# Batch 0's first feed-forward phase: w_in's first quarter in two loads, norms ahead of q's second part, single token tiles

## The chip, the cores and the metric

The kernel runs on one core of one Trainium2 chip. Times are microseconds (us) measured on the device, the whole program each time. The runs of one experiment were made together on one chip, experiments 2 and 3 on other chips than 1 and 4, so times are compared within an experiment. A profile is one such execution with every instruction recorded; its span is 1.7 to 2.1 us shorter than the time of the same run.

Names in the profile: PE is TensorE's matmuls and PEld its weight loads, DVE is VectorE, ACT is ScalarE, POOL is GpSimd (which here mostly issues loads). L453 is a line of the kernel; the changed kernel and most experiments have the same line a few numbers later (L456), as lines were added above it.

## The reference, cut to what matters

```python
def phi(x):                                     # elu(x) + 1
    return np.where(x > 0, x, np.exp(x) - 1.0) + 1.0
q_p, k_p = phi(q), phi(k)                       # batch 8, heads 8, seq 576, head_dim 64
kv  = np.einsum('bhsd,bhse->bhde', k_p, v)
z   = np.sum(k_p, axis=2)
num = np.einsum('bhsd,bhde->bhse', q_p, kv)
den = np.einsum('bhsd,bhd->bhs', q_p, z)[..., None] + 1e-06
x   = (num / den)  # -> (4608, 512)
h   = x @ w_in                                  # 512 x 2048
g   = h * (1 / (1 + np.exp(-beta * h)))
out = g @ w_out                                 # 2048 x 512
```

## The kernel before

It works batch by batch. For each batch, linear attention gives x, transposed to xT. The "H phase" multiplies xT by w_in and puts a silu on the result; the "y phase" multiplies by w_out. PE runs batch 0's H and y phases while batch 1's attention is prepared between their matmuls. Everything is in a fixed order that the program gives. The loads all go through one queue that GpSimd issues:

```python
    load_nine(k9, k)
    load_nine(q9, q, j1=4)
    ...                                         # batch 0's v
    load_nine(q9, q, j0=4)
    for i in range(4):
        nc.gpsimd.dma_start(out=w_in_sb[i], in_=w_in_v[:, :, i * 512 : (i + 1) * 512])
    load_w_out(0)
    load_w_out(1)
    load_k(1)
    load_q(1)
    ...
    load_w_out(2)
    load_v(1)
    load_w_out(3)
```

The start of batch 0's H phase, and the plan of what is slipped in after which group (a group is four matmuls: one 128-wide slice ff of w_in's columns times token tiles t0 to t1):

```python
    exp0(0, 4, N9)
    relu0(0, 4, N9)
    silu_table()
    num_norm(0, 0)                              # VectorE: den, reciprocal, multiply -> xs
    phi0(0, 4, 6)
    warm(4)                                     # matmuls on zeros
    x_trans(0, 0, dve=True)                     # PE transposes xs, VectorE copies it to xT
    qb2 = att_banks(BF16)
    q_trans0(2, qb2, 0)
    q_out0(2, qb2, 0, False)
    num_norm(0, 1)
    phi0(0, 6, N9)
    ...
    h_phase(
        0, xT[0],
        [(ff, 0, 1) for ff in range(4)] + [(ff, 1, 2) for ff in range(4)]
        + [(ff, 0, 2) for ff in range(4, 8)] + [(ff, 2, 4) for ff in range(8)]
        + [(ff, 0, 4) for ff in range(8, 12)],
        {
            3: [F(x_trans, 0, 1), F(num_mm, 0, 2), F(num_norm, 0, 2), F(q_rest0)],
            5: [F(num_mm, 0, 3), F(num_norm, 0, 3)],
            7: [F(x_trans, 0, 2)],
            8: [F(num_mm, 0, 4), F(num_norm, 0, 4)],
            9: [F(x_trans, 0, 3), F(tidy0)],
            12: [F(x_trans, 0, 4)],
            17: [F(w_out_scale, 0), F(w_out_scale, 1)],
        },
    )
```

And what comes after it:

```python
    h_last(0, xT[0], [])                        # the last four ff of the H phase
    ...
    exp_(1, 1); exp_(1, 0)                      # ScalarE, batch 1's k and q
    silu_table()
    relu(1, 1); relu(1, 0)                      # VectorE from here
    w_out_scale(2)
    phi(1, 1)                                   # the minimum, k
    v_copy(1)                                   # vaug <- vraw: needs v(1)'s load
    phi(1, 0)                                   # the minimum, q
    y_phase_wide(0, {
        ...
        9: [F(kv_mm, 1), F(kv_evac, 1), F(w_out_scale, 3)],
        10: [F(q_trans, 1, 0, 1, wide=True), F(q_trans, 1, 2, 3, wide=True)],
        ...
    })
```

## Time and profile before

| | |
|---|---|
| time, median of 3 | 296.88 us (296.63 to 297.01) |
| span of the profile | 295.1 us |
| PE busy | 285.1 us, 97% |
| first matmul of the H phase | 17.09 us |
| first matmul of the y phase | 34.09 us |
| batch 1's kv matmuls start | 42.82 us |

Here is VectorE at the start of the H phase, from the instructions in order of time (start in us, length in us, engine, line, what it writes and reads; in brackets the idle time before it and what ended it). The first norm (den, rden, xs) starts only when relu0, the first row, is done, although its own inputs were there; that is the order the change turns round.

```profile
13.76 0.65 DVE L264 TENSOR_SCALAR r<-xqk 128x1280 bf16<-128x1280 bf16 x1 [0.55 <-DMA xqk<-in_q_dram]
14.45 0.17 DVE L413 TENSOR_SCALAR den<-att 128x8 f32<-128x8 f32 x1
14.88 0.69 DVE L415 TENSOR_TENSOR xs<-att,rden 128x512 bf16<-128x512 f32 x1
16.07 0.42 DVE L370 COPY xT<-mm 128x512 bf16<-128x512 bf16 x1 [0.16 <-PE mm L433]
```

And two lines of the waits of PE and its weight loads (total us, times, longest): the wait that the change is after, and one, much smaller in the list.

```profile
PE mm L453 <- DMA w_in<-in_moe_w_in_dram: 0.8, 1, 0.8
PEld L344 <- DVE vaug L370: 0.4, 1, 0.4
```

### The profile page before, as it was taken

Reading aid. Unit: us, or ns where it says so; the run is one execution under the profiler, and the core shown is the slowest. Engines: PE = TensorE matmul, PEld = TensorE weight load, DVE = VectorE, ACT = ScalarE, POOL = GpSimd, SP = SyncE. Lnnn points to the kernel's source line nnn. Section 1 sums busy time; section 2 is a strip of 40 time slices with the busy share of each in tenths; the row PEclk is TensorE's granted clock in tenths of the full one; section 3 lists DMA queues with packets and bytes.
Section 4 is the critical chain, followed back from the end, with each engine's and each line's share of the span. In section 5 each row is a group of like instructions: output and inputs, shape, how many; then the busy total and the mean of one; then the engine's idle time right before and its main releaser. Section 6 shows DMA issues by size and latency. Waiting matters only on the chain.

```text
span 295.1 us, 4791 instructions
## 1 busy us (share of the span) xinstructions
PE 285.1 (97%) x1911; PEld 144.9 (49%) x1932; DVE 125.2 (42%) x264; ACT 175.5 (59%) x234; POOL 52.2 (18%) x72
## 2 busy tenths in 40 slices
PE   8979999999999999999999999999999999999994
PEld 2557445644565544445444544454445444444443
DVE  5675388504772174616461646164715400110012
ACT  2798786889988770778077808790770077018500
POOL 8925475544006000320020000000000000000000
PEclk9999999999999999999999999999999999999998
DMA  7999999999939943698357445024502400120032
GB/s 109 189 205 344 255 273 192 257 193 190 164 142 150 180 93 98 130 177 151 98 128 79 73 116 126 2 72 115 127 0 73 117 36 0 38 94 13 2 71 71
DMA packets 69719, 36.43 MB, mean 123 GB/s; under 512 B 38321, under 2 KB 64193, under 8 KB 69697
## 3 DMA queue, kind: packets, MB, share of 16 engines
q0 software_dynamic: 38912, 20.45, 47.7%
q1 hardware_dynamic: 30624, 15.55, 21.0%
q8 instruction: 15, 0.25, 0.4%
q10 hardware_dynamic: 160, 0.13, 0.2%
q14 instruction: 8, 0.06, 0.0%
HBM read 36.71 MB, written 9.44 MB: 156 GB/s over the span
## 4 chain that ended last, share of the span: by engine, by line
PE 71%; DMA 17%; ACT 4%; POOL 4%; issue 3%; DVE 0%; POOLq 0%; ACTq 0%
PE mm L453 33%; PE mm L505 32%; DMA xqk<-in_q_dram 9%; DMA vraw<-in_v_dram 4%; DMA w_in<-in_moe_w_in_dram 4%; PE att L399 2%; ACT e L229 2%; POOL xqk L131 1%; PE att L344 1%; PE mm L537 1%; ACT L229 1%; POOL vraw L131 1%; ACT g L445 1%; POOL w_in L159 1%; ACT L445 0%
## 5 line engine op out<-in xcount | busy, mean ns | idle before, releaser
L445 ACT ACTIVATE g<-mm,beta_c 128x512 bf16<-128x512 f32 (+2 forms) x156 | 97.3, 633 | 88.1 <-PE mm L453 87.8
L505 PE MATMUL mm<-w_out,g 128*128 128x512 bf16 x541 | 127.2, 379 | 1.2 <-issue 0.3
L453 PE MATMUL mm<-xT,w_in 128*128 128x512 bf16 (+2 forms) x560 | 107.8, 349 | 1.2 <-DMA w_in<-in_moe_w_in_dram 0.8
L453 PEld LDWEIGHTS <-w_in 128*128 128x128 bf16 x656 | 62.0, 98 | 62.0 <-DMA w_in<-in_moe_w_in_dram 1.0
L505 PEld LDWEIGHTS <-g 128*128 128x128 bf16 x560 | 52.7, 98 | 57.3
L515 DVE COPY y_sb<-mm 128x512 f32<-128x512 f32 x27 | 18.7, 692 | 70.4 <-PE mm L505 67.4
L229 ACT ACTIVATE e<-xqk 128x2560 bf16<-128x2560 bf16 x14 | 31.9, 2329 | 0.1
L415 DVE TENSOR_TENSOR xs<-att,rden 128x512 bf16<-128x512 f32 (+1 forms) x40 | 27.6, 689 | 1.6 <-DVE rden L414 0.2
L242 DVE TENSOR_TENSOR qk_p<-r,e 128x2560 bf16<-128x2560 bf16 x14 | 20.9, 1490 | 13.1 <-ACT e L229 12.4
L355 DVE CAST kv_bd<-att 64x130 bf16<-64x130 f32 x28 | 8.2, 292 | 34.5 <-PE att L344 34.1
L72 POOL DMA_DIRECT2D vraw<-in_v_dram x7 | 6.8, 972 | 77.4 <-DVE vaug L370 70.9
L413 DVE TENSOR_SCALAR den<-att 128x8 f32<-128x8 f32 (+1 forms) x40 | 6.5, 162 | 27.0 <-PE att L399 26.8
L399 PEld LDWEIGHTS <-q_pT 128*128 128x128 bf16 (+1 forms) x160 | 11.7, 100 | 10.7 <-DVE xs L415 2.1
L399 PE MATMUL att<-kv_bd,q_pT 128*128 128x130 bf16 (+1 forms) x160 | 15.8, 221 | 1.1 <-DVE kv_bd L370 0.7
L453 PE MATMUL mm<-xT_tail,w_in 128*128 128x512 bf16 x63 | 13.9, 379 | 0.1
L237 DVE TENSOR_SCALAR r<-xqk 128x2560 bf16<-128x2560 bf16 x14 | 11.9, 858 | 3.9 <-DMA xqk<-in_q_dram 2.3
L572 PE MATMUL mm<-g 128*128 128x512 bf16 x34 | 10.4, 468 | 1.2 <-DVE g L143 1.2
L72 POOL DMA_DIRECT2D xqk<-in_k_dram x7 | 8.0, 1150 | 10.2 <-ACT e L229 3.6
L229 ACT ACT_TABLE_LOAD x7 | 9.0, 1283 | 0.1
L414 DVE RECIPROCAL rden<-den 128x8 f32<-128x8 f32 (+1 forms) x40 | 8.1, 201 | 1.4
L72 POOL DMA_DIRECT2D xqk<-in_q_dram x7 | 6.5, 924 | 6.9 <-ACT g L445 2.1
L256 ACT ACTIVATE e<-xqk 128x1280 bf16<-128x1280 bf16 (+1 forms) x4 | 4.4, 1154 | 5.1 <-DMA xqk<-in_k_dram 4.6
(72 smaller groups left out, 142.5 us busy)
## 6 DMA issues: line engine op xcount, KB each, us to landing
out_dram<-y_sb SPq DMA_DIRECT2D x28, 256.0 KB, 2.3
xqk<-in_k_dram POOLq DMA_DIRECT2D x7, 512.0 KB, 10.7
xqk<-in_q_dram POOLq DMA_DIRECT2D x7, 512.0 KB, 11.8
vraw<-in_v_dram POOLq DMA_DIRECT2D x7, 512.0 KB, 11.5
w_in<-in_moe_w_in_dram POOLq DMA_DIRECT2D x4, 512.0 KB, 11.3
g<-in_moe_w_out_dram POOLq DMA_DIRECT2D x4, 512.0 KB, 10.9
out_dram<-y_sb SPq DMA_DIRECT2D x14, 128.0 KB, 5.1
xqk<-in_moe_w_out_dram POOLq DMA_DIRECT2D x2, 512.0 KB, 14.3
```

Source lines behind the costliest of these rows:

```text
L72: eng.dma_start(out=dst[:, :, 0:NJ, :].rearrange("p h j d -> p h (j d)"), in_=src[b, :, 0:MAIN, :].rearrange("h (p j) d -> p h (j d)", j=NJ),)
L229: nc.scalar.activation(st[b, "e", a][:, h0:h1], xqk[b % NX][:, a, h0:h1], ACTF.Exp)
L237: nc.vector.tensor_scalar(st[b, "r", a][:, h0:h1], xqk[b % NX][:, a, h0:h1], 0.0, 1.0, ALU.max, ALU.add)
L242: nc.vector.tensor_tensor(st[b, "p"][:, a].rearrange("p j (h d) -> p h j d", h=H)[:, h0:h1], st[b, "r", a][:, h0:h1], st[b, "e", a][:, h0: ...
L355: nc.vector.tensor_copy(kv_bd[b % 2][i][gs, :, g, :], st[b, "kvp"][gs, 2 * i : 2 * i + 2, :])
L399: nc.tensor.matmul(nps[:n, p // 2, c0 : c0 + 2 * (D + 1)], st[b, "qT"][:, t, p, :n], kv_bd[b % 2][p // 2][:, p % 2], start=True, stop=True ...
L415: nc.vector.tensor_mul(xs[:n], nv[:, :, :, 0:D], rden[:n, :, :, None].to_broadcast([n, 2, 4, D]))
L445: nc.scalar.activation(g_sb[b % 2][:, ff, c0:c1], hp[:, c0:c1], ACTF.Silu, scale=beta_c[:, ff : ff + 1],)
L453: nc.tensor.matmul(hp[:, c0:c1], w_in_sb[ff // 4][:, kc, (ff % 4) * P : (ff % 4 + 1) * P], x[:, t0:t1, kc, :] if b < B else x[:, kc, c0:c1 ...
L505: nc.tensor.matmul(yp, g_sb[b % 2][:, ff, t * P : (t + 1) * P], w_out_sb[ff // 4][:, ff % 4, :], start=(ff == 0), stop=(ff == FC - 1),)
L515: nc.vector.tensor_copy(y_sb, yp)
L572: nc.tensor.matmul(st["warm"], g_sb[0][:, FC - 1, 0:P], g_sb[0][:, FC - 1, :], start=True, stop=True, skip_group_check=True,)
```

## The change

The intent: PE stood still for 0.88 us for the first norm and 0.84 us for w_in. So load half a quarter of w_in first, let VectorE do the norm ahead of relu, move q's second part (which would hold PE, ScalarE and VectorE up ahead of the first H matmuls) into the H phase, and take the last token tiles later and one by one, so that H groups never wait for two tiles at once. The diff, cut to its core:

```diff
-    for i in range(4):
-        nc.gpsimd.dma_start(out=w_in_sb[i], in_=w_in_v[:, :, i * 512 : (i + 1) * 512])
+    for f0, f1 in ((0, 256), (256, 512), (512, 1024), (1024, 1536), (1536, 2048)):
+        i, c0 = f0 // 512, f0 % 512
+        nc.gpsimd.dma_start(
+            out=w_in_sb[i][:, :, c0 : c0 + f1 - f0], in_=w_in_v[:, :, f0:f1]
+        )
...
     exp0(0, 4, N9)
-    relu0(0, 4, N9)
     silu_table()
     num_norm(0, 0)
-    phi0(0, 4, 6)
+    relu0(0, 4, N9)
     warm(4)
     x_trans(0, 0, dve=True)
-    qb2 = att_banks(BF16)
-    q_trans0(2, qb2, 0)
-    q_out0(2, qb2, 0, False)
+    warm(2)
     num_norm(0, 1)
-    phi0(0, 6, N9)
+    phi0(0, 4, 6)
...
-        + [(ff, 0, 2) for ff in range(4, 8)] + [(ff, 2, 4) for ff in range(8)]
+        + [(ff, 0, 2) for ff in range(4, 8)] + [(ff, 2, 3) for ff in range(4)]
+        + [(ff, 3, 4) for ff in range(4)] + [(ff, 2, 4) for ff in range(4, 8)]
         + [(ff, 0, 4) for ff in range(8, 12)],
         {
-            3: [F(x_trans, 0, 1), F(num_mm, 0, 2), F(num_norm, 0, 2), F(q_rest0)],
-            5: [F(num_mm, 0, 3), F(num_norm, 0, 3)],
-            7: [F(x_trans, 0, 2)],
-            8: [F(num_mm, 0, 4), F(num_norm, 0, 4)],
-            9: [F(x_trans, 0, 3), F(tidy0)],
-            12: [F(x_trans, 0, 4)],
-            17: [F(w_out_scale, 0), F(w_out_scale, 1)],
+            3: [F(x_trans, 0, 1, dve=True), F(phi0, 0, 6, N9), F(q_second0)],
+            5: [F(num_mm, 0, 2), F(num_norm, 0, 2), F(q_rest0)],
+            8: [F(num_mm, 0, 3), F(num_norm, 0, 3)],
+            9: [F(x_trans, 0, 2)],
+            10: [F(num_mm, 0, 4), F(num_norm, 0, 4), F(tidy0)],
+            12: [F(x_trans, 0, 3)],
+            15: [F(x_trans, 0, 4)],
+            25: [F(w_out_scale, 0), F(w_out_scale, 1)],
         },
```

`q_second0` holds the three lines about `qb2`.

More of the change, by code (lines that the diff above doesn't have):

```diff
@@ L636, in tidy0, with q_second0 @@
         nc.vector.memset(vraw[0][TAIL:P, :, NJ, :], 0.0)
+    def q_second0():
+        st["qb2"] = att_banks(BF16)
+        q_trans0(2, st["qb2"], 0)
+        q_out0(2, st["qb2"], 0, False)
     def q_rest0():
+        qb2 = st["qb2"]
         q_trans0(3, qb2, 256)
```

## The prediction

> **What bounds the kernel now.** I read the page's first part, then the chain that ended last, then each engine's instructions in order of time from 13 to 46 us, where the change acts, and last the windows of DMA traffic. One core, so no dies to compare; PEclk is 9 or 10 tenths throughout.
>
> ```profile
> PE 285.1 (97%) x1911; PEld 144.9 (49%) x1932; DVE 125.2 (42%) x264; ACT 175.5 (59%) x234; POOL 52.2 (18%) x72
> PE 71%; DMA 17%; ACT 4%; POOL 4%; issue 3%; DVE 0%; POOLq 0%; ACTq 0%
> ```
>
> PE is busy 97% of the span, and the chain is PE 71%, its last 213 us (from 82.1) nearly all matmuls back to back. All of the change lies before 34 us, so it can pay only if PE reaches the unchanged part earlier and nothing there makes it wait again. The start, PE:
>
> ```profile
> 13.73 1.02 PE L572 MATMUL mm<-g 128*128 128x512 bf16 x4
> 15.63 0.40 PE L433 MATMUL mm<-identity,xs 128*128 128x128 bf16 x4 [0.88 <-DVE xs L415]
> 17.09 1.07 PE L453 MATMUL mm<-xT,w_in 128*128 128x128 bf16 x16 [0.84 <-DMA w_in<-in_moe_w_in_dram]
> 19.21 0.61 PE L453 MATMUL mm<-xT,w_in 128*128 128x128 bf16 x8 [0.31 <-ACT xT L372]
> 19.93 0.39 PE L399 MATMUL att<-kv_bd,q_pT 128*128 128x130 bf16 x4
> 24.12 6.68 PE L453 MATMUL mm<-xT,w_in 128*128 128x256 bf16 x44
> 34.09 8.80 PE L505 MATMUL mm<-w_out,g 128*128 128x512 bf16 x39
> ```
>
> Columns are start, length, what, and the idle time before it with its releaser. The first H group waits 0.84 us for the whole first quarter of w_in; its input tile was ready earlier (copy 16.07 to 16.49). This H phase runs from 17.09 to 34.09, 17.0 us, of which its matmuls alone are 64 x 215.5 ns = 13.8 us. Next, what meets PE after that:
>
> ```profile
> 41.88 0.83 DVE L370 COPY vaug<-vraw 128x2560 bf16<-128x2560 bf16 x1 [0.94 <-DMA vraw<-in_v_dram]
> 42.62 1.48 DVE L242 TENSOR_TENSOR qk_p<-r,e 128x2560 bf16<-128x2560 bf16 x1
> 44.02 1.20 DVE L355 CAST kv_bd<-att 64x130 bf16<-64x130 f32 x4
> 42.82 0.82 PE L344 MATMUL att<-vaug,qk_p 128*64 128x65 bf16 x40
> 44.45 0.61 PE L380 MATMUL att<-identity,qk_p 128*128 128x128 bf16 x8
> 45.28 0.62 PE L380 MATMUL att<-identity,qk_p 128*128 128x128 bf16 x8 [0.22 <-DVE kv_bd L355]
> ```
>
> This is the main finding. Batch 1's kv matmuls start at 42.82, just after the copy of v(1) ends at 42.71, and that copy waited 0.94 us for v(1)'s **load**. PE without that wait would be there at 34.09 + 40 x 0.2155 = 42.71. So PE and the loads arrive together to about 0.1 us. From the copy on, VectorE runs without a gap (copy, minimum, kv_bd eviction), and PE waits for that eviction at 45.28. PE's schedule from 45.28 on is therefore set by when v(1) lands, not by when the H phase ended.
>
> v(1)'s landing is set by the traffic. In the windows from 12 us to 42 us the DMA part shows all slices at 9, and the landings come in issue order: w_in's quarters are seen at POOL's releases at 17.34, 19.76, 22.35 and 24.88, some 2.55 us each. The queue is never empty: POOL issues v(1) at 28.88 and it lands about 41.8.
>
> **What the Trainium skill says.** (1) "ScalarE: Activation LUTs", What ACT_TABLE_LOAD costs: an ACTIVATE with one pointer operand takes about 280 ns + 0.833 ns per column, back-to-back ones overlap by 93 ns, a table load takes about 1283 ns. The trace has 0.69 us for a 512-wide silu (page: 0.71), 0.47 for 256 (0.49), four of 128 in 1.14, and 1.28 for the table load: it agrees. So narrow groups are dear on ScalarE. (2) "TensorE: Matmul & The Clock Gate", Wait — 56ns, not 53.3ns?: warm matmuls follow at 55.6 ns for 128 columns and 215.7 for 512. Here 16 of 128 columns take 0.91 us to the next instruction, 57 ns each: narrow groups are cheap on PE. (3) "DMA: Bandwidth & Descriptors", Specifications: line rate needs 512 B or more. Half a quarter has rows of 256 bf16, 512 B, just at that limit; k's main load has the same rows. (4) "Trainium Kernel Development and Optimization", Best Practices, point 5: matmul busy share is a poor measure. Agreed here: PE reads 5.00 of 5.00 us between 20 and 25, though the steps below find about 0.5 us of waiting there.
>
> **The change part by part.**
>
> *w_in's first quarter in two loads.* The first half should land one half of 2.55 us before the whole did, about 15.8; the second at 17.1 or slightly later. From the packets' starts, 1,024 B packets of w_in pass at about 100 per 0.5 us and 512 B packets of k(1) at about 194. So 1,024 half-size packets take 2.64 us and 512 whole ones 2.55: everything behind comes **0.09 us later**. One more issue of 0.75 us on POOL is hidden, with several loads queued.
>
> *The norm ahead of relu.* The first norm waited behind relu0 (13.76 to 14.45); its own inputs were ready at about 13.7. Now den starts there, xs is ready at 13.7 + 1.12 + 0.06 = 14.87 instead of 15.63. But relu (0.65 us) now stands between xs and the copy to xT, so that copy starts at about 15.4 and the H matmuls could start at 15.9 instead of 16.55. The first half of w_in is there.
>
> *The H groups.* ff 0 and 1 of tile 0 run at 15.90 to 16.36. Then ff 2 needs the **second** half: 17.15. So ff 0 to 3 end at 17.15 + 2 x 0.228 = 17.61 instead of 18.00. Of the 1.2 us earlier start only 0.4 survive.
>
> *q's second part* moves into the H phase: 8 small transposes, 0.2 us of PE, earlier done in the wait for w_in. xT's second copy on VectorE ends at 18.46 instead of 19.15; the second tile starts at about 18.5 instead of 19.21, a gain of 0.7. Then num_mm of tile 2 and q's rest (0.38 + 0.30) stand ahead of its last two groups. num_mm of tile 3 waits for the last q copy, since its PSUM buffer is that of the q transposes (in the trace it starts at 19.93 as that copy ends at 19.92); in the new order that is about 20.65. I follow PE, ScalarE and VectorE step by step this way with the durations above (a silu every 0.25, 0.39, 0.62 us for 128, 256, 512 columns; a copy to xT 0.47). At the end of ff 7 of tiles 0 and 1 PE is at 22.8, against 23.1 in the same walk through the kernel before, which had also done one more transposition of 0.23. The lead is gone.
>
> *Single token tiles.* Four groups of 256 columns become eight of 128. PE: 4 x (2 x 0.228 - 0.432) = +0.10 us. ScalarE: 4 x (2 x 0.2525 - 0.39) = **+0.46 us**. Between 23 and 25.5 ScalarE owes eight silus of 0.25 and copies of 0.47 and 0.38, 2.9 us, for PE work of 8 x 0.228 + 0.45 = 2.3. With four PSUM banks shared by groups and transposes, PE then waits for a bank, about 0.6 us in all.
>
> *The sum for the H phase.* The walk ends at 33.89 for the kernel before (measured 34.09) and at 34.30 for the changed one: the phase ends **0.4 us later**, near 34.5, with PE at the kv matmuls at about 43.12, 0.30 late. w_out_scale sits later in the plan but holds the same place in VectorE's order, and waits for loads anyway: nothing.
>
> *What of it reaches the end.* A late kv ends at about 43.94; VectorE is free for the eviction only at 44.02 + 0.09. The 0.30 fits into the 0.34 (44.02 - 43.68) that lay there. What is left is the 0.09 of the loads. 296.88 + 0.09 = **296.97**.
>
> **The rivals.** *A: the early start carries through.* For it: the two waits 0.88 and 0.84 vanish in part. If the second half landed soon enough, or my bank waits were wrong, PE would leave the H phase up to 0.6 us earlier. Against it: v(1) lands when it lands, so at most about 0.1 us comes through, 296.8. Only if v(1)'s landing moved too could more be had, to about 296.3. *B: ScalarE becomes the bound in the single-tile stretch and PE is later than I find.* Each 0.1 us past the slack goes straight to the end. With an H phase 0.9 us longer, the time would be about 297.4. For it: four PSUM banks, and xT copies queued behind silus. Against: VectorE took one copy away from ScalarE. *C: the halves slow the traffic* by more than packet counts say, a pause between two transfers of say 0.3 us (a guess): everything behind it, v(1) included, shifts, 297.2. *D: a gain or loss over 2%*, 5.9 us: PE's waits in the changed stretch amount to some 2.5 us, so a gain of that size is not there to have; a loss would need a new wait longer than any named here.
>
> **Range and chances.** The three runs of before span 0.4 us. My centre is 297.0. Downwards there is only A and noise: 296.4. Upwards B and C: 297.7. Faster by over 2%: 0.01; slower: 0.01; within 2%: 0.98.
>
> **What would show each step right or wrong.** First H matmul near 15.9, and an idle PE of about 0.8 us before ff 2, released by w_in near 17.1. If ff 2 starts by 16.5, the two-halves step is wrong. PE waiting on ScalarE or on banks between 23 and 26, and the first matmul of L505's successor (y) near 34.5: if it is at 34.1 or earlier, the ScalarE step is wrong. v(1)'s copy on VectorE at 41.9 to 42.0 and the kv_bd eviction at 44.1: if that copy moves earlier by more than 0.2, the main finding is wrong. From the second pair of q transposes (45.28 before) to the end, the same length to 0.2 us. The prediction fails if PE's lateness exceeds the slack, or if later waits between 45 and 82 us turn out to hang on the H phase itself.

## The result, and the profile after

The changed kernel took 297.56 us (median of 4, 296.85 to 298.03) against 296.94 for the kernel before (296.63 to 297.04). Ratios here are the mean time of one kernel's fast runs over that of the other's of the same rounds, so not quite the ratio of the medians: 1.002, 95% interval 0.9998 to 1.0043. It was run twice more: 297.21 against 296.66 (ratio 1.0012, 0.9994 to 1.003), and 296.91 against 296.87 (0.9999, 0.9986 to 1.0013). The same within 2%, and not told apart from no change at all.

At this size the record itself sets a limit. Each run's span is recorded beside its time, and what lies outside the span is 1.72 to 1.84 us in the kernel before and 1.87 to 1.98 us in the changed one. So over 0.1 us of what separates their times lies outside anything that a profile shows, and its cause is open.

The profile of the changed kernel has a span of 296.1 us. Its page and chain, for the two lines that the prediction opens with:

```profile
PE 286.1 (97%) x1929; PEld 145.7 (49%) x1950; DVE 125.0 (42%) x265; ACT 175.5 (59%) x237; POOL 53.7 (18%) x73
PE 70%; DMA 22%; ACT 2%; issue 2%; POOL 1%; DVE 0%; POOLq 0%
```

PE in the changed stretch, in order of time:

```profile
15.70 0.40 PE L436 MATMUL mm<-identity,xs 128*128 128x128 bf16 x4
16.62 0.61 PE L456 MATMUL mm<-xT,w_in 128*128 128x128 bf16 x8
18.26 0.62 PE L456 MATMUL mm<-xT,w_in 128*128 128x128 bf16 x8 [1.03 <-DMA w_in<-in_moe_w_in_dram]
19.62 0.62 PE L456 MATMUL mm<-xT,w_in 128*128 128x128 bf16 x8 [0.30 <-DVE xT L373]
35.42 8.80 PE L508 MATMUL mm<-w_out,g 128*128 128x512 bf16 x39
```

The wait for the norm is gone, and the first two groups (16.62, eight matmuls) start ahead of w_in's second half. Then PE waits 1.03 us for that half. And PE, VectorE around batch 1's kv:

```profile
42.94 0.83 DVE L373 COPY vaug<-vraw 128x2560 bf16<-128x2560 bf16 x1 [0.63 <-DMA vraw<-in_v_dram]
43.68 1.48 DVE L245 TENSOR_TENSOR qk_p<-r,e 128x2560 bf16<-128x2560 bf16 x1
45.09 1.20 DVE L358 CAST kv_bd<-att 64x130 bf16<-64x130 f32 x4
44.15 0.82 PE L347 MATMUL att<-vaug,qk_p 128*64 128x65 bf16 x40
45.78 1.18 PE L383 MATMUL att<-identity,qk_p 128*128 128x128 bf16 x16
```

Everything here lies 1.06 us later than in the kernel before (the copy of v(1) at 42.94 against 41.88), and so does the end: 296.1 against 295.1. But most of this run's delay is older than the change. The first exp waits for batch 0's k, the first load of all. These two rows are that exp (with the two that follow it) in the kernel before and, below it, in the changed one:

```profile
6.81 3.16 ACT L256 ACTIVATE e<-xqk 128x1280 bf16<-128x1280 bf16 x3 [4.57 <-DMA xqk<-in_k_dram]
```

```profile
7.98 3.17 ACT L259 ACTIVATE e<-xqk 128x1280 bf16<-128x1280 bf16 x3 [5.75 <-DMA xqk<-in_k_dram]
```

k landed 1.17 us later here, though up to that point the two programs issue the same loads in the same order. So the first question was whether that is chance, and the second what the change costs when it is taken out.

One reading of all 14 profiles carries the rest. In each of them the time from the start of the kv_bd eviction (VectorE's copy of what the kv matmuls gave) to the end of the span is between 250.97 and 251.17 us. So in these runs whatever happened before that eviction reached the end only through the moment when it started.

### The profile page after: what moved, and what is told of

Same layout as the page of the kernel before. It is cut to its first block, busy times and chain, and to the rows that moved or that the text cites. A ratio compares the mean times of both kernels' runs of the same rounds, so it can differ in the third digit from the quotient of the medians.

```text
span 296.1 us, 4832 instructions
## 1 busy us (share of the span) xinstructions
PE 286.1 (97%) x1929; PEld 145.7 (49%) x1950; DVE 125.0 (42%) x265; ACT 175.5 (59%) x237; POOL 53.7 (18%) x73
## 4 chain that ended last, share of the span: by engine, by line
PE 70%; DMA 22%; ACT 2%; issue 2%; POOL 1%; DVE 0%; POOLq 0%
PE mm L456 33%; PE mm L508 32%; DMA xqk<-in_q_dram 9%; DMA vraw<-in_v_dram 5%; DMA w_in<-in_moe_w_in_dram 4%; DMA xqk<-in_k_dram 4%; PE att L402 2%; PE att L347 1%; PE mm L540 1%; POOL xqk L131 1%; ACT e L232 1%; ACT g L448 1%; ACT L232 0%; ACT L581 0%; PE att L436 0%
## 5 line engine op out<-in xcount | busy, mean ns | idle before, releaser
L72 POOL DMA_DIRECT2D xqk<-in_k_dram x7 | 6.9, 982 | 9.2 <-ACT e L232 4.4
```

The lines of the kernel that those rows point to most:

```text
L72: eng.dma_start(out=dst[:, :, 0:NJ, :].rearrange("p h j d -> p h (j d)"), in_=src[b, :, 0:MAIN, :].rearrange("h (p j) d -> p h (j d)", j=NJ),)
```

## The experiments

The theory: the eviction starts at the later of two moments, v(1)'s copy plus 2.14 us (copy and second minimum on VectorE without a gap) or the start of the kv matmuls plus 0.87 us. The first hangs on the loads, the second on PE's H phase; the end is 251.05 us later. The rivals: PE alone sets the end; or the halved load slows the traffic; or ScalarE with its single tiles makes PE later than the slack allows. The constants were read from the first six profiles; the other eight are a test of them.

### 1. Both kernels again, and the change with and without its load

The first two are the kernels as they are. The third is the kernel before with only this:

```diff
-    for i in range(4):
-        nc.gpsimd.dma_start(out=w_in_sb[i], in_=w_in_v[:, :, i * 512 : (i + 1) * 512])
+    for f0, f1 in ((0, 256), (256, 512), (512, 1024), (1024, 1536), (1536, 2048)):
+        ...
```

The fourth is the changed kernel with these lines turned back.

> The kernel before, unchanged, as a control. Theory S (start jitter): the changed kernel's profile shows the first k load 1.2 us later than the kernel before (first exp at 7.98 against 6.81 us) although nothing ahead of it differs; so the moment the first exp starts varies from run to run, and this profile may show anything from 6.8 to 8.0, with the end moving with it. Time 296.6 to 297.1 if only this kernel's usual spread holds. Rival C2 (the change causes the late start, for instance through where things lie in memory or one more queued load): here the first exp starts at 6.8 to 6.9 and the spread of the five times stays below 0.5 us.

> The changed kernel, unchanged, to size the spread. Theory S: median within 0.4 us of the kernel before, first exp anywhere from 6.8 to 8.0; in its profile the copy of v(1) and everything after it moves with the load stream, and the time from that copy to the end is the same 253.2 us as in the first two profiles (295.1 - 41.88 and 296.1 - 42.94). Rival C2: first exp again near 8.0 and a median 0.5 us or more above the kernel before.

> The kernel before with w_in's first quarter in two loads and nothing else. Prediction's step: the traffic behind it comes 0.09 us later, so 297.0. Rival C (the halves slow the traffic by more): 297.2 to 297.6, and the spacing from the first half's landing to the second's is well over 1.3 us. The H matmuls of ff 0 and 1 start as soon as the first half is there (16.5), ff 2 waits for the second.

> The changed kernel with w_in's first quarter in one load. Theory of the prediction: 296.9, since its later H phase (0.4 us) is still swallowed before the kv_bd eviction. If the halves were what costs 0.6 us (rival C), this is at the kernel before or below; if the order of the H phase costs it (rival B), this stays at 297.5.

| kernel | median us | ratio to before (95%) | first exp | w_in complete, matmuls go on | first y matmul | v(1)'s copy | kv matmuls | eviction | span |
|---|---|---|---|---|---|---|---|---|---|
| before, first profile | 296.88 | | 6.81 | 17.09 | 34.09 | 41.88 | 42.82 | 44.02 | 295.1 |
| before again | 296.84 | 1.0003 (0.9982 to 1.0025) | 7.38 | 17.12 | 34.11 | 41.75 | 42.84 | 43.89 | 294.9 |
| changed, first profile | 297.56 | 1.002 (0.9998 to 1.0043) | 7.98 | 18.26 | 35.42 | 42.94 | 44.15 | 45.09 | 296.1 |
| changed again | 297.21 | 1.0012 (0.9994 to 1.003) | 7.19 | 17.45 | 34.62 | 41.87 | 43.34 | 44.21 | 295.2 |
| only the two loads | 297.01 | 1.0006 (0.9989 to 1.0024) | 6.93 | 17.12 | 33.66 | 41.90 | 42.79 | 44.05 | 295.1 |
| changed, one load | 297.05 | 1.001 (0.9992 to 1.0027) | 6.96 | 16.78 | 34.39 | 42.48 | 43.37 | 44.63 | 295.6 |

What follows. The late first load is not the change's doing. The two profiles of the kernel before have the first exp at 6.81 and 7.38, the first two of the changed one at 7.98 and 7.19; in experiment 2 a variant of the kernel before has it at 8.05. So rival C2 falls as to the load. The times are less clean: 297.21 is 0.55 us above the 296.66 of the kernel before in these rounds, where I had expected no more than 0.4 and C2 at least 0.5; but the same kernel's other runs beside it, as a control, had 296.84. 11 runs of the kernel before in these rounds spread from 296.29 to 298.12.

From the moment w_in is complete to the first y matmul the kernel before takes 17.00 and 16.99 us, the changed one 17.16 and 17.17. With only the two loads it is 16.54: that part alone does bring PE 0.4 us ahead. Nor do the halves slow the traffic as rival C has it: w_in is complete at 17.12, as in the control, and v(1)'s copy starts at 41.90, against 41.88 and 41.75. The halves did come 2.55 us apart, one of C's marks, but because the first landed sooner. Yet the kernel with only the two loads is not faster, since its copy of v(1) starts at 41.90 as before, and the kv matmuls at 42.79. PE could have been there at 33.66 + 8.62 = 42.28 (8.62 us are forty y matmuls of 215.5 ns); it waits 0.5 us instead (by the profile's own record of idle PE, 0.33):

```profile
42.79 0.82 PE L347 MATMUL att<-vaug,qk_p 128*64 128x65 bf16 x40 [0.33 <-DVE vaug L373]
```

In the second profile of the changed kernel it is the other way round: kv at 43.34 + 0.87 = 44.21, the eviction's start, while v(1)'s copy would have allowed 44.01. Here the later H phase came through with 0.2 us:

```profile
41.87 0.83 DVE L373 COPY vaug<-vraw 128x2560 bf16<-128x2560 bf16 x1 [0.35 <-DMA vraw<-in_v_dram]
42.61 1.49 DVE L245 TENSOR_TENSOR qk_p<-r,e 128x2560 bf16<-128x2560 bf16 x1
44.21 1.21 DVE L358 CAST kv_bd<-att 64x130 bf16<-64x130 f32 x4
```

The fourth run takes the two halves of the change apart. With one load and the new order the stretch is 17.61 us (16.78 to 34.39). So the two loads take 0.46 us off it and the new order with its single tiles adds 0.61; that comes to 0.15, and the whole change measures 0.17. Its median, 297.05, lies between the 296.9 that I had expected and the 297.5 of rival B; in its profile v(1) set the eviction (42.48 + 2.14 = 44.62, measured 44.63).

### 2. The last tiles in pairs again; more and fewer loads ahead of v(1)

First, the changed kernel with its last quarter's groups joined:

```diff
-        + [(ff, 0, 2) for ff in range(4, 8)] + [(ff, 2, 3) for ff in range(4)]
-        + [(ff, 3, 4) for ff in range(4)] + [(ff, 2, 4) for ff in range(4, 8)]
+        + [(ff, 0, 2) for ff in range(4, 8)] + [(ff, 2, 4) for ff in range(8)]
...
-            12: [F(x_trans, 0, 3)],
-            15: [F(x_trans, 0, 4)],
-            25: [F(w_out_scale, 0), F(w_out_scale, 1)],
+            11: [F(x_trans, 0, 3)],
+            13: [F(x_trans, 0, 4)],
+            21: [F(w_out_scale, 0), F(w_out_scale, 1)],
```

> The changed kernel with the last quarter's token tiles in pairs again (8 groups of 256 columns, no single tiles there), everything else of the change kept. Read from the profile: the length from the release of w_in's second half to the first y matmul. The kernel before has 17.00 and 16.99 us from its only w_in release, the changed one 17.16 and 17.17. ScalarE step (four groups split cost 0.46 us of ScalarE and bank waits on PE): 16.7 or less here. Rival (the splitting is free, the extra comes from the order of q's second part): 17.1 or more. Time about 297.0 either way, as the eviction of batch 1's kv_bd decides.

Second, the kernel before with an idle load ahead of v(1):

```diff
     load_w_out(2)
+    nc.gpsimd.dma_start(out=pad, in_=w_out_v[:, 10:12, :])     # a buffer nobody reads
     load_v(1)
```

> The kernel before with one more load of 512 KB that nobody reads, ahead of v(1). In all six profiles so far the time from the start of the kv_bd eviction to the end of the span is 250.97 to 251.08 us, and that eviction starts 2.14 us after the copy of v(1) starts. If v(1)'s landing sets the end, one load of 1.29 us more moves the copy to about 43.2, the eviction to 45.3 and the time to 298.1. If PE sets the end (rival A), the load is hidden: 296.8.

Third and fourth, both kernels with one load of the same size left out. Their outputs are wrong, which doesn't matter for the times.

```diff
+    nc.vector.memset(w_out_f[2][1], 0.0)                       # at the start
...
-    load_w_out(2)
+    nc.gpsimd.dma_start(out=w_out_f[2][0], in_=w_out_v[:, 8:10, :])
     load_v(1)
```

> The kernel before with half of w_out's third quarter not loaded (filled with zeros at the start, so a wrong result on purpose): v(1) lands 1.29 us sooner. The eviction then starts when kv's matmuls are done, 0.87 us after their start, which PE reaches by itself at the first y matmul + 8.62 = 42.72. Theory: eviction at 43.6, time 296.3 to 296.5, 0.4 less, and no more than that. If PE were not waiting for v(1) at all: 296.8. If the loads were all: 295.6.

> The same lighter loads (wrong result on purpose) in the changed kernel. Theory: the eviction waits for PE, first y matmul (34.6) + 8.62 + 0.87 = 44.1, so the time stays near 297.0, some 0.5 us above the same kernel without the change, since here nothing hides the later H phase. If the H phase is not later in truth and only the landing differs, it comes down to 296.4 like the other.

| kernel | median us | ratio to before (95%) | first y matmul | v(1)'s copy | kv matmuls | eviction | span |
|---|---|---|---|---|---|---|---|
| pairs | 297.18 | 0.9995 (0.998 to 1.0011) | 34.84 | 42.37 | 43.56 | 44.52 | 295.6 |
| before, one load more | 298.06 | 1.0026 (1.001 to 1.0042) | 34.07 | 43.28 | 44.16 | 45.43 | 296.5 |
| before, one load less | 296.21 | 0.9962 (0.9945 to 0.998) | 33.72 | 41.08 | 42.45 | 43.60 | 294.6 |
| changed, one load less | 296.93 | 0.9996 (0.9974 to 1.0019) | 34.09 | 41.08 | 42.82 | 43.68 | 294.7 |

The kernel before had a median of 297.26 in these rounds (296.56 to 298.21). They were run on another chip.

One load more: VectorE's rows show the copy released by v(1) after 2.14 us of idling, and the eviction 2.15 us behind it, as expected. PE had nothing to do with it: its first y matmul was at 34.07, and it could have been at the kv matmuls at 42.69. So a microsecond of loads ahead of v(1) does reach the end.

```profile
43.28 0.83 DVE L371 COPY vaug<-vraw 128x2560 bf16<-128x2560 bf16 x1 [2.14 <-DMA vraw<-in_v_dram]
45.43 1.20 DVE L356 CAST kv_bd<-att 64x130 bf16<-64x130 f32 x4
```

One load less: the changed kernel's eviction now waits for PE, in so many words:

```profile
41.08 0.83 DVE L374 COPY vaug<-vraw 128x2560 bf16<-128x2560 bf16 x1
43.68 1.21 DVE L359 CAST kv_bd<-att 64x130 bf16<-64x130 f32 x4 [0.37 <-PE att L348]
```

With the loads out of the way the two kernels come apart: 296.21 against 296.93, and no run of the one (296.04 to 296.52) reaches the lowest of the other (296.80). Not all of these 0.72 us belong to the H phase. The median span is 294.4 against 294.8; the rest lies outside the span (1.8 us against 2.1). So where v(1) doesn't hide it, the change costs about 0.4 us of span, and the rule gives 0.37 for it (43.32 against 43.69). The two profiled runs differ by only 0.1 us of span because the first was one of the slower ones of its kernel.

In the kernel before, the eviction started at 43.60 as I had written, but not for my reason. PE would have allowed 42.45 + 0.87 = 43.32; VectorE's copy took 1.20 us here instead of 0.83, and the second minimum ran to the eviction without a gap. GpSimd had begun to issue a load 0.30 us before the copy, at 40.78, and took 0.88 us for it, as it does with nothing beside it. An issue beside the copy does not alone explain it: in the changed kernel with a load less one began 0.16 us before the copy, and there the copy took 0.83 and the issue 1.46. That one of the two holds up the other, and which does hangs on how far ahead the issue began, would fit; no run tests it.

```profile
41.08 1.20 DVE L371 COPY vaug<-vraw 128x2560 bf16<-128x2560 bf16 x1
42.20 1.47 DVE L243 TENSOR_TENSOR qk_p<-r,e 128x2560 bf16<-128x2560 bf16 x1
43.60 1.20 DVE L356 CAST kv_bd<-att 64x130 bf16<-64x130 f32 x4
```

Pairs: my expectation failed. In this run w_in's second half came in time for PE, so I compare from the first group of the second tile, which by luck starts at 18.52 both here and in the changed kernel's third profile (told of below). PE with pairs, then PE in the changed kernel:

```profile
18.52 0.62 PE L456 MATMUL mm<-xT,w_in 128*128 128x128 bf16 x8 [0.29 <-DVE xT L373]
24.11 1.03 PE L456 MATMUL mm<-xT,w_in 128*128 128x256 bf16 x8 [0.83 <-ACT xT L375]
34.84 1.24 PE L508 MATMUL mm<-w_out,g 128*128 128x512 bf16 x5
```

```profile
17.15 0.62 PE L456 MATMUL mm<-xT,w_in 128*128 128x128 bf16 x8 [0.64 <-DMA w_in<-in_moe_w_in_dram]
18.52 0.62 PE L456 MATMUL mm<-xT,w_in 128*128 128x128 bf16 x8 [0.30 <-DVE xT L373]
22.45 0.83 PE L456 MATMUL mm<-xT,w_in 128*128 128x256 bf16 x8
24.37 0.27 PE L436 MATMUL mm<-identity,xs 64*128 64x64 bf16 x4
34.32 1.89 PE L508 MATMUL mm<-w_out,g 128*128 128x512 bf16 x8
```

With pairs PE waits 0.83 us for the copy of the fourth tile, as a pair needs both tiles; it reaches y after 16.32 us, the changed kernel after 15.80 (15.80 to 15.81 in all five profiles with this H phase and two loads). So, by one profile of the pairs, the single tiles gain 0.5 us in this order: they fill the wait for a tile with work on the one before. They are needed only because the tiles come later in the new plan.

### 3. v(1) earlier

If v(1)'s landing is the wall, load it earlier. Nothing is left out here; the second half of w_out's third quarter goes behind v(1), and ScalarE scales that half.

```diff
-    load_w_out(2)
-    load_v(1)
+    nc.gpsimd.dma_start(out=w_out_f[2][0], in_=w_out_v[:, 8:10, :])
+    load_v(1)
+    nc.gpsimd.dma_start(out=w_out_f[2][1], in_=w_out_v[:, 10:12, :])
     load_w_out(3)
...
     exp_(1, 0)
+    w_out_scale(2, dve=False, c0=2)            # c0, c1: which of the four slices
     silu_table()
...
-    w_out_scale(2)
+    w_out_scale(2, c1=2)
```

It was put on the kernel before, on the kernel before with the two loads, and on the changed kernel.

> The kernel before with v(1) loaded ahead of the second half of w_out's third quarter (nothing left out, result right), and that half scaled on ScalarE after the second exp instead of on VectorE. Theory: the eviction no longer waits for v(1); it waits for the last of kv's matmuls (first y matmul + 8.62 + 0.87, 43.6) or for the second minimum, so it starts near 43.6, the span is 294.6 and the time 296.2 to 296.5, as with the lighter loads. Rival: the late half of w_out now stops PE at the eleventh y group, or ScalarE's two scalings delay the copies of q, and the time is 296.8 or more.

> The same with w_in's first quarter in two loads (the one part of the change that shortened the H phase: first y matmul at 33.66 with ff 2's release at 17.12, 16.54 us against 17.00). Theory: eviction at 33.66 + 8.62 + 0.87 = 43.15, span 294.2, time 295.8 to 296.0, the best of all kernels. If something else than PE and v(1) holds the eviction (the second minimum, behind ScalarE's second exp), it stays at 43.5 and 296.3.

> The changed kernel with v(1) loaded early in the same way. Theory: PE's later H phase is no longer hidden: eviction near 34.4 + 8.62 + 0.87 = 43.9 to 44.1, time 296.6 to 297.0, 0.3 to 0.7 above the kernel before with the same loads. If the H phase of the changed kernel costs nothing, 296.3.

| v(1) early on | median us | ratio to before (95%) | first y matmul | v(1)'s copy | kv matmuls | eviction | span |
|---|---|---|---|---|---|---|---|
| before | 296.53 | 0.9988 (0.9975 to 1.0002) | 33.58 | 40.58 | 42.31 | 43.17 | 294.3 |
| before with two loads | 296.73 | 0.9989 (0.9977 to 1.0002) | 34.04 | 40.80 | 42.77 | 43.63 | 294.8 |
| changed | 296.62 | 0.999 (0.9978 to 1.0003) | 34.46 | 41.02 | 43.19 | 44.05 | 295.1 |

The kernel before had 297.14 in these rounds (296.69 to 297.33). They were run on another chip. In all three the eviction waits for PE, 0.86 us after the kv matmuls start. For the first of them:

```profile
40.58 0.87 DVE L370 COPY vaug<-vraw 128x2560 bf16<-128x2560 bf16 x1 [0.35 <-DMA vraw<-in_v_dram]
41.37 1.47 DVE L242 TENSOR_TENSOR qk_p<-r,e 128x2560 bf16<-128x2560 bf16 x1
43.17 1.21 DVE L355 CAST kv_bd<-att 64x130 bf16<-64x130 f32 x4 [0.33 <-PE att L344]
```

All three are 0.4 to 0.6 us below the kernel before of the same rounds, and each interval still touches 1, so I call it likely, not shown. The second one missed: I had expected 43.15 and the best time of all. In its profile batch 0's q landed later (its exp at 14.13 against 13.60 in the first), so the H matmuls began at 16.89 against 16.44. And the first does not wait for w_in's one load either, so in this pair the two loads had nothing to gain. The third had its eviction at 44.05, as expected, but not the time: 296.62 is 0.09 above the first, where I had expected 0.3 to 0.7. The median spans, 294.8 and 294.6, are 0.2 apart. Here the change costs less than with a load less, and the profiled pair (295.1 and 294.3) shows more than the medians do.

### 4. The changed kernel a third time

> The changed kernel a third time, for the size of the difference and one more profile. If the end is the later of two things, v(1)'s copy + 2.14 us and PE's arrival at the kv matmuls + 0.87 us, plus 251.05 us, then this profile's span follows from those two starts to 0.1 us. The median should be 0.1 to 0.5 us above the kernel before of the same rounds. A median 0.6 us or more above it would mean that the change delays the landing of v(1) itself, one at or below it that the later H phase is hidden in most runs.

296.91 us (296.87 to 297.2) against 296.87, ratio 0.9999: 0.04 above, less than the 0.1 to 0.5 expected and not quite the "at or below" that would have meant hidden in most runs. The profile: v(1)'s copy at 42.05, kv matmuls at 43.05. The rule gives 42.05 + 2.14 = 44.19 or 43.05 + 0.87 = 43.92, the later is 44.19; measured 44.20, and span 295.2. The later H phase was hidden in this run. Over the 14 profiles the rule gives the eviction to 0.02 us in 13; the one it misses, by 0.28, is the kernel before with a load less, whose copy took 1.20 us.

## Why the prediction was right

The predicted time was 297.0 with a range of 296.4 to 297.7; the three medians are 297.56, 297.21 and 296.91. The time alone tests little: the kernel before's own medians in the five sets of runs, 296.66 to 297.26, lie in that range too, and the 0.09 us that the centre rests on is far below the spread. What tests the working are its steps in the profiles:

*The main finding held.* PE's schedule from the eviction on is fixed up to the end, 250.97 to 251.17 us in 14 profiles, and the eviction follows v(1)'s landing unless PE is late by more than the slack. The extra load showed the first half of it, the missing one and the early v(1) the second.

*w_in in two loads.* The waiting at the second half was as predicted: in the third profile PE goes on at 17.15, the predicted moment. The 0.09 us of slower traffic can't be seen in a spread of a microsecond; it stays open. The first half landed sooner than I had said, in most runs: in the eight profiles with two loads GpSimd's issue that waits for it starts at 14.81 to 15.94 (15.94 in the run with the latest k), and the halves lie up to 2.7 us apart in place of 1.3. It did no harm, as the first tile was ready only at 15.9.

*The norm first.* First H matmul predicted at 15.9; measured 15.91 and 15.78 in the two profiles of the changed kernel without a late k.

*The walk through the H phase.* In the third profile, whose w_in release is the predicted 17.15: second tile at 18.52 (predicted 18.5), ff 7 ended at 22.88 (22.8), first y matmul at 34.32 (the walk 34.30). The waits for banks and copies on PE between 23 and 31 us add up to 0.53 us (0.6). Mis-sized was the difference to the kernel before: I took 0.4 from two walks, though the walk had already fallen 0.2 short of the kernel before as measured (33.89 against 34.09). Against the measured one the H phase is 0.17 us longer.

*Single tiles.* This is the step whose reasoning failed. I told them as a loss (0.10 us on PE, 0.46 on ScalarE) and did not ask what pairs would do in the new order. There the same groups in pairs are 0.5 us slower. ScalarE's busy time is indeed a little higher with single tiles, 175.5 or 175.6 us against 175.3, but PE does not pay for it on balance.

*What of it reaches the end.* Predicted: nothing of the H phase, 0.09 of the loads. In two of three profiles of the changed kernel the eviction was indeed set by v(1); in the other PE's lateness came through with 0.2 us. By the prediction's figures PE would have been 0.12 us ahead of what v(1) allows (43.99 against 44.11); it was 0.06 and 0.27 ahead and once 0.20 behind. That v(1) decided in the very profile of the result was therefore partly luck. The slack of 0.34 us is there only while loads and PE keep the distance of the one profile that I had read it from, and from run to run they shift against each other by some tenths.

*What I did not foresee* is the spread. I took 0.4 us of it from three runs; 11 runs of the kernel before then covered 1.8 us. In the first profile of the changed kernel the first load, w_in and v(1) were all late by 1.06 to 1.17 us, which is most of why that run took 298.03. But a late first load does not always stay: with the first exp at 7.93 and 8.05 w_in's first quarter was complete by 16.84, no later than elsewhere. And the changed kernel with one load began at 6.96 and still had v(1) 0.6 us late. Where the delays arise is open; no run here changes it, and the runs without a profile show nothing of it.

*The skill's pages.* The walk took the trace's 0.25 us for a narrow silu. By "ScalarE: Activation LUTs", What ACT_TABLE_LOAD costs, four of 128 columns back to back come to 1.27 us (an estimate from the page: 4 x 0.387 less 3 x 0.093) where the trace has 1.14, so "it agrees" was too generous for narrow ones; for 256 and 512 columns it holds to 0.02 us. "DMA: Bandwidth & Descriptors", Specifications, puts line rate at 512 B and more; rows of just 512 B showed no slowing that these runs could tell from noise. One reading of the page of the profile was loose too: PEclk is 9 tenths or more only up to the last slice, which has 8.

## What to carry to other kernels

A wait on the busiest engine is worth only what the next wall leaves of it: before shortening it, look downstream for the first place where that engine meets something that keeps its own time, here a load, and read how far apart the two arrive, in more than one profile. When several tenths are at stake, find an interval that is the same in every profile and measure what comes ahead of it in pieces; that told more in single profiles than five rounds of timing. Splitting a load helps only up to the first use of its second part, and work for the wait must come from elsewhere: here the two loads alone took 0.46 us off the H phase, and the time stayed the same, as v(1) came no sooner.

## What the Trainium skill lacked or had wrong

- "DMA: Bandwidth & Descriptors" tells how long one transfer takes, but not how far the landings in one queue vary from run to run: the first load's user started between 6.68 and 8.05 us in 14 profiles of programs that issue the same loads up to there. In one pair of profiles such a delay was still there at v(1), 35 us later (1.17 us at the first load, 1.06 at v(1)); in others it was gone by w_in's first quarter.
- The same page has no word on two loads queued one behind the other landing unevenly: two halves of one quarter of w_in, 1.3 us of traffic each, were seen 1.3 to 2.7 us apart by the engine that issues loads.
- "SBUF — State Buffer", Terms, says that VectorE and GpSimd arbitrate for one pair of ports and that the loser blocks. Its figures for it, two slow-downs of 6.8 and 1.5 times under Who interferes with whom, are not for a load's issue beside a copy. Some profiles would fit that one of the two waits: with an issue begun 0.30 us before it the copy of 128 x 2560 bf16 took 1.20 us and the issue 0.88; with one begun 0.10 to 0.16 us before (three profiles) the copy took 0.83 and the issue 1.41 to 1.47. No run was made to show that this is the cause.
